# Attention and mixture of adapters in one kernel: the order of the work written out as one list

## The chip, the cores and the metric

The kernel runs on one core of a Trainium2 chip. The core has a matrix engine (PE, with its weight loads shown apart as PEld), a vector engine (DVE), a scalar engine (ACT), GpSimd (POOL) and SyncE (SP), which only issues DMAs here; sixteen DMA engines move data. Each engine works through its own instructions strictly in order, and semaphores order engines against each other. The metric is the device time of one execution in microseconds. Matmuls write to PSUM, from where DVE or ACT copy ("evict") to SBUF.

## The reference

```
q, k, v: 8 batches x 8 heads x 576 rows x 64
phi(x)  = [max(x,0) * cos(pos), max(x,0) * sin(pos)]          # 128 features
kv      = phi(k)^T v            (per batch and head, 128 x 64)
z       = sum of phi(k) over the rows
attn    = (phi(q) kv) / (phi(q) z + 1e-6)
x       = attn as 4608 tokens x 512
logits  = x @ w_gate            (8 experts)
w       = softmax over the two largest logits
out     = x + sum over those two of w * ((x @ A[e]) @ B[e])   # rank 16
```

## The kernel before, in words

The 4608 tokens are cut into 36 tiles of 128. Nine tiles (`NS` is 9) belong to two batches: four to the first, one, the mixed tile, half to each, four to the second. A batch's k, q and v each come with one DMA that also turns float32 into bfloat16; these loads are issued on POOL's queue, except the first k, which SP issues. There are five buffers each for q and v; from batch 5 on, k, q and v reuse the earlier ones.

Work per batch: 9 columns s of k are scaled by the cosine and the sine (18 products `kp`), on DVE (L153), ACT (L151) or POOL (L156). DVE and ACT take the maximum with 0 in the same instruction; for POOL's columns DVE applies it beforehand, in place (`relu_k`, L165), and POOL waits for that. `kv` (L180) then adds up the 9 columns in two PSUM tiles `cd`, 8 matmuls a column, and `kv_out` (L188) copies the sum to SBUF.

Work per tile n: `transp_q` transposes and scales q by matmuls with diagonal matrices, as 16 matmuls (L213), or for some tiles as 32 small ones ("quad", L201); `evac_q` evicts the two halves with the maximum (L229 on ACT, L231 on DVE). `numden` (L257) multiplies them with kv into the one PSUM tile `nd`; 1e-6 is added by two small matmuls (L252), or, where `eps_dve(n)` says so, by DVE in `normalise` (L268). `normalise` takes the reciprocal (L270) and multiplies (L277) into `xt`. `transp_x` (L285) transposes `xt` into the PSUM tile `xz`, `evac_x` (L291) copies it to SBUF as `xT`, `logits` (L311) multiplies it with A and w_gate. `nd` and `xz` are single: the next tile's `numden` waits for this tile's multiplication, the next `transp_x` for this tile's copy.

Work per group of three tiles: `gate_a` (L320 to L328) finds the two largest logits, `gate_sig` (L337) takes a sigmoid on ACT, `gate_b` (L344, L346) weights the rank-16 products into `zg`; `transp_z` (L359) transposes them into the second half of `xz`, and they are copied with the next xT, or by `evac_z`. Then for each tile `delta` adds two products in PSUM, x itself (L377) and the adapters' part (L382); `evac_o` (L408 on ACT, L410 on DVE) copies to `osb`, which has 24 buffers, and `store` issues one DMA on SP (two for a mixed tile). In `delta_add` (L397, L402) x is added by POOL in SBUF, in place of the product L377.

The order is that of the Python program, since the framework keeps each engine's instructions in the order written. A loop over the tiles writes one fixed pattern per tile; tables filled ahead of it (`kv_at`, `relu_at`, `pool_at`, `act_at`, `dve_at`, `early_at`, `late_at` and others) say at which tile a column, a relu or a group's step is written. For batches 2 to 7 all of POOL's columns of one batch stand in one block behind the relus that they need, and the loads of later batches behind that block: k of b+3, q of b+2, v of b+3. The small DMA `first_loads` on SP reads one row of the last batch's k; every store stands behind it on SP's queue, and the last batch's relu, which overwrites that buffer, waits for it.

Of the kernel before, what the change touches and what calls it, by code (L numbers as in the profile page):

```python
# [15 lines left out]
EPS = 1e-6  # L16


@with_exitstack
def kernel(ctx, tc, q, k, v, w_gate, A, Bw, out):  # L20
# [169 lines left out]
    def quad(n):  # L190
        return n >= 27

    def transp_q(n):
# [14 lines left out]
        for gp in range(2):  # L208
            qpT_t[n, gp] = t = qd.tile([128, 2, 4, HALF], FP32, name="qd", tag="qd")
            for j, (b, s) in enumerate(tokens(n)):  # L210
                for gi in range(2):
                    for i, cols in enumerate((lo, hi)):
                        nc.tensor.matmul(out=t[cols, j, 2 * gi:2 * gi + 2, :],  # L213
                                         lhsT=q_b[b][:, 2 * gp + gi, s, :], rhs=diag[:, s, i],
                                         start=(j == 0 and gi == 0), stop=True,
                                         skip_group_check=True)
# [16 lines left out]
    def move_q(n):  # L233
        transp_q(n)
        evac_q(n, 0)
        evac_q(n, 1)

    def eps_dve(n):

        return n > 13 and n in kv_at  # L240
# [46 lines left out]
    def evac_x(n, g=None):  # L287
# [3 lines left out]
        nc.vector.tensor_copy(t[:, 0:c], xz[:, 0:c * 128].rearrange("p (c s) -> p c s", c=c))  # L291
# [69 lines left out]
    def evac_z(g, parts):  # L361
        zgT_t[g] = t = p_g.tile([128, 3, 128], BF16, name="zgT")
        for eng, i, j in parts:
            if eng == "act":
                nc.scalar.copy(t[:, i:j], zT_ps(g)[:, i:j])
            else:
                nc.vector.tensor_copy(t[:, i:j], zT_ps(g)[:, i:j])
# [16 lines left out]

    def delta(n, own=True):
        delta_x(n, own)
        delta_z(n)

    def delta_add(n, own=True):

        if own:
            dx = cd[dx_n[0] % 2]
            dx_n[0] += 1
        else:
            dx = qd.tile([128, DM], FP32, name="dx", tag="qd")
        g = group_of[n]
        nc.tensor.matmul(out=dx, lhsT=zgT_t[g][:, n - groups[g][0], :], rhs=Ball,  # L397
                         start=True, stop=True)
        osb_t[n] = dx
        evac_o(n)  # L400
# [22 lines left out]

    kv_at, relu_at, pool_at, act_at, dve_at = {}, {}, {}, {}, {}

    def put(at, step, what):
        at.setdefault(step, []).append(what)

    for s in range(NS):
        for i in range(2):  # L430
            put(act_at if s % 2 == 0 and s < 8 else dve_at, 1 if s < 4 else 2, (1, s, i))
    kv_at[2] = [(1, s) for s in (1, 0, 3, 2)]
    kv_at[3] = [(1, s) for s in (5, 4, 7, 8, 6)]
    for b in range(2, B):
        first = b // 2 * NS + b % 2 * 4
        at = {2: 5, 3: 8, 4: 12, 5: 17, 6: 20, 7: 23}[b]
        n_pool = {2: 5, 3: 7, 4: 8, 5: 8}.get(b, 9)
        for s0, s1 in ((0, 3), (3, n_pool)):
            put(relu_at, at, (b, s0, s1))
        for s in range(n_pool):  # L440
            put(pool_at, at, (b, s))
        for i in range(2):
            if n_pool <= 7:
                put(dve_at, at, (b, 7, i))
            if n_pool < 9:
                put(act_at, first - 4 + i, (b, 8, i))
            if n_pool == 5:
                put(act_at, first - 3 + i, (b, 6, i))
                put(act_at, first - 2, (b, 5, i))
        order = (7, 0, 1, 2, 3, 4, 8, 6, 5) if n_pool <= 7 else (0, 1, 2, 3, 4, 5, 8, 6, 7)  # L450
        if n_pool == 9:
            order = range(NS)
        for j, s in enumerate(order):

            if b == 2:
                ahead = 2 if j < 4 else 1
            elif b == 3:
                ahead = 3 if j < 2 else 2 if j < 5 else 1
            else:
                ahead = 4 - min(j // 2, 3)  # L460
            put(kv_at, first - ahead, (b, s))

    early_at, late_at, gate_a_at, gate_b_at, move_at = {}, {}, {}, {}, {}
    prev = 5
    for g, t in enumerate(groups[:-2]):
        at = max(t[-1] + 1, prev + 1)
        for n in t:
            if t[-1] + 1 < at or (n < t[-1] and prev == at - 1):  # L470
                put(late_at, at - 1, n)
            else:
                put(early_at, max(n + 1, at - 1), n)
        prev = at + 1
        put(gate_a_at, at, g)
        put(gate_b_at, at + 1, g)
        put(move_at, at + 2, g)
    put(late_at, NT - 2, NT - 3)

    with tc.manual_schedule():  # L480
# [19 lines left out]
        load_v(3)  # L500
        load_k(4)
        load_q(3)
# [7 lines left out]
        g10, g11, g12 = range(len(groups) - 3, len(groups))  # L510
        todo, held = [], []
        first_loads = persist.tile([1, 8], BF16, name="first_loads")

        def emit(d, own=True, eng="act", add=False):
            if add:
                delta_add(d, own)
            else:
                delta(d, own)
                evac_o(d, eng)
            if held is None:  # L520
                store(d)
            else:
                held.append(d)

        for n in range(NT - 1):
            if n > 0:
                g = move_at.get(n - 1, (None,))[0]
                evac_x(n - 1, g)
                if g is not None:
                    todo += groups[g]  # L530
            normalise(n)
            if n != 3:
                move_q(n + 1)
            for b, s in kv_at.get(n, ()):
                kv(b, s)
                if kv_n[b] == NS:
                    kv_out(b)
            for t in early_at.get(n, ()):
                logits(t)
            if n == 3:  # L540
                move_q(n + 1)
            for g in gate_a_at.get(n, ()):
                gate_a(g)
            for g in gate_b_at.get(n, ()):
                gate_b(g)
            now = todo[:2 if len(todo) > 3 and n not in kv_at else 1]
            del todo[:len(now)]
            for d in now:
                emit(d, n not in kv_at, add=n > 27)
            for g in gate_a_at.get(n, ()):  # L550
                gate_sig(g)
            transp_x(n)
            for g in move_at.get(n, ()):
                transp_z(g)
            for b, s, i in dve_at.get(n, ()):
                scale_k1(b, s, i, "dve")
            for b, s0, s1 in relu_at.get(n, ()):
                relu_k(b, s0, s1)
            for b, s in pool_at.get(n, ()):
                scale_k(b, s)  # L560
                if (b, s) == pool_at[n][-1]:
                    if b + 3 < B:
                        load_k(b + 3)
                    if b + 2 < B:
                        load_q(b + 2)
                    if b + 3 < B:
                        load_v(b + 3)
                    if b + 3 == B - 1:

                        nc.sync.dma_start(out=first_loads, in_=k_b[B - 1][0:1, 0, 0, 0:8])  # L570
                        for d in held:
                            store(d)
                        held = None
            for t in late_at.get(n, ()):
                logits(t)
            numden(n + 1)
            for b, s, i in act_at.get(n, ()):
                scale_k1(b, s, i, "act")


        evac_x(NT - 2)
        normalise(NT - 1)
        transp_z(g10)
        logits(NT - 2)
        evac_z(g10, [("act", 0, 3)])
        todo += groups[g10]
        for d in todo[:-3]:
            emit(d)
        transp_x(NT - 1)
        gate_a(g11)  # L590
        emit(todo[-3])
        gate_sig(g11)
        evac_x(NT - 1)
        logits(NT - 1)
        gate_b(g11)
        emit(todo[-2])
        gate_a(g12)
        transp_z(g11)
        evac_z(g11, [("act", 0, 2)])
# [36 lines left out]
```

## Time and profile before

| | |
|---|---|
| median of 3 runs | 114.68 us (114.47 to 114.92) |
| the profiled execution | 114.54 us |
| its span, first to last instruction | 112.8 us |
| granted PE clock | 0.996 |
| read from HBM, written to it | 28.85 MB, 9.44 MB |

In the profile, a row of a group reads: line, engine, operation, output<-inputs, shapes and count, then busy time in us, mean ns of one, and the idle time before it with what ended it. A row of the timeline reads: start in us, length in us, engine, line, operation, and in brackets idle time before it. A row with "x2" covers two instructions; starts can lie closer together than lengths, since an engine begins an instruction before the last has quite ended. In the chain of waits a row is a start, a length and what ran or was waited for.

### The profile page before, as it was taken

The page shows a single profiled execution, that of the slowest core. Times are in us where ns is not written, and L with a number is a line of the kernel's source. Part 1 is how long each engine was busy: PE and PEld are TensorE (multiplying, and loading weights), DVE is VectorE, ACT ScalarE, POOL GpSimd, SP SyncE. Part 2 cuts the span into 40 slices and gives each one's busy share as a digit, 9 for nine tenths or more (in the row PEclk, how much of TensorE's full clock was granted, in tenths as well). Part 3 has the DMA queues.
Part 4 walks back from the last instruction along what each step waited for, and adds up shares of the span by engine and source line. Part 5 has one row for each costly group of instructions (what it writes and reads, how often), then busy time and mean ns, then how long its engine had stood idle before and what let it go on. Part 6 is the DMA issues. An engine that isn't in the chain of part 4 may idle for free.

```text
span 112.8 us, 4956 instructions
## 1 busy us (share of the span) xinstructions
PE 96.1 (85%) x2050; PEld 74.1 (66%) x2068; DVE 83.7 (74%) x296; ACT 78.2 (69%) x169; POOL 72.3 (64%) x134
## 2 busy tenths in 40 slices
PE   2999676978899899999999999998998997978710
PEld 1347465867796788868788888785786886754200
DVE  5598489459969677695987998999949589786620
ACT  5087579755986595797876978856777777895720
POOL 5992223228995996299939999989980445774000
PEclk9999999999999999999999999999999999999998
DMA  2999999999999999999999999999999424526892
GB/s 41 385 206 208 213 202 210 210 180 208 208 208 209 207 209 209 209 206 213 204 207 208 208 209 208 242 348 383 381 324 366 142 100 97 185 101 226 285 340 82
DMA packets 19670, 24.77 MB, mean 220 GB/s; under 512 B 2624, under 2 KB 14528, under 8 KB 19648
## 3 DMA queue, kind: packets, MB, share of 16 engines
q0 software_dynamic: 13856, 13.84, 73.8%
q1 hardware_dynamic: 5792, 10.62, 26.9%
q8 instruction: 16, 0.26, 0.9%
q14 instruction: 6, 0.05, 0.1%
HBM read 28.85 MB, written 9.44 MB: 340 GB/s over the span
## 4 chain that ended last, share of the span: by engine, by line
PE 40%; DMA 28%; DVE 15%; issue 4%; POOL 4%; ACT 4%; POOLq 0%; DVEq 0%; ACTq 0%
DMA k<-in_k_dram 14%; DMA v<-in_v_dram 12%; PE cd L180 9%; PE za L311 7%; PE qd L213 6%; PE xz L285 5%; PE nd L257 4%; DVE xt L277 4%; PE dx L377 3%; DVE k L165 3%; DVE xT L291 2%; DVE zg L346 2%; ACT osb L408 2%; PE qd L201 2%; DMA out_dram<-osb 2%
## 5 line engine op out<-in xcount | busy, mean ns | idle before, releaser
L229 ACT ACTIVATE qpT<-qd 128x512 bf16<-128x512 f32 x71 | 38.6, 595 | 15.0 <-PE qd L213 10.9
L156 POOL TENSOR_SCALAR kp<-k,cos_tab 128x256 bf16<-128x256 bf16 x46 | 22.6, 490 | 7.1 <-DVE k L165 6.5
L277 DVE TENSOR_TENSOR xt<-nd,rden 128x512 bf16<-128x512 f32 x36 | 24.9, 691 | 1.3
L291 DVE COPY xT<-xz 128x512 bf16<-128x512 bf16 (+1 forms) x36 | 17.1, 476 | 9.9 <-PE xz L359 6.4
L156 POOL TENSOR_SCALAR kp<-k,sin_tab 128x256 bf16<-128x256 bf16 x46 | 21.9, 476 | 0.0
L180 PE MATMUL cd<-v,kp 64*128 64x128 bf16 x576 | 20.3, 217 | 0.9 <-DVE kp L153 0.9
L285 PEld LDWEIGHTS <-xt 128*128 128x128 bf16 x144 | 10.8, 115 | 12.1 <-DVE xt L277 7.9
L285 PE MATMUL xz<-ident,xt 128*128 128x128 bf16 x144 | 14.4, 222 | 5.0 <-DVE xt L277 4.3
L180 PEld LDWEIGHTS <-kp 64*128 64x128 bf16 x576 | 16.3, 94 | 3.1 <-issue 0.9
L257 PE MATMUL nd<-kvsb,qpT 128*128 128x65 bf16 (+1 forms) x320 | 16.7, 195 | 1.1 <-DVE qpT L231 0.5
L213 PE MATMUL qd<-diag,q 128*64 128x128 bf16 x432 | 17.3, 222 | 0.3 <-DMA q<-in_q_dram 0.3
L402 POOL TENSOR_TENSOR osb<-osb,xt 128x512 f32<-128x512 f32 x8 | 9.2, 1160 | 9.6 <-ACT osb L408 8.0
L408 ACT COPY osb<-dx 128x512 f32<-128x512 f32 x19 | 11.2, 588 | 5.9 <-remote 2.1
L213 PEld LDWEIGHTS <-q 128*64 128x64 bf16 x432 | 13.1, 109 | 1.8 <-DMA q<-in_q_dram 0.5
L257 PEld LDWEIGHTS <-qpT 128*128 128x128 bf16 (+1 forms) x320 | 12.7, 100 | 1.9 <-ACT qpT L229 0.7
L311 PE MATMUL za<-AW,xT 128*128 128x144 bf16 x140 | 12.4, 227 | 0.7 <-DVE zg L346 0.5
L311 PEld LDWEIGHTS <-xT 128*128 128x128 bf16 x144 | 9.0, 98 | 3.2 <-DVE xT L291 1.0
L408 ACT COPY osb<-cd 128x512 f32<-128x512 f32 x16 | 9.1, 597 | 1.3 <-PE cd L382 1.3
L62 POOL DMA_DIRECT2D v<-in_v_dram x8 | 6.2, 778 | 5.2 <-DMA q<-in_q_dram 4.4
L485 PE MATMUL wu<-wide,ones 128*128 128x512 bf16 x24 | 7.3, 477 | 2.0 <-DVE AW L115 2.0
L62 POOL DMA_DIRECT2D q<-in_q_dram x8 | 6.1, 763 | 3.6 <-DMA k<-in_k_dram 3.6
L62 POOL DMA_DIRECT2D k<-in_k_dram x7 | 5.4, 771 | 3.9 <-DMA k<-in_k_dram 2.2
(75 smaller groups left out, 133.8 us busy)
## 6 DMA issues: line engine op xcount, KB each, us to landing
out_dram<-osb SPq DMA_DIRECT2D x32, 256.0 KB, 3.9
v<-in_v_dram POOLq DMA_DIRECT2D x8, 576.0 KB, 16.5
q<-in_q_dram POOLq DMA_DIRECT2D x8, 576.0 KB, 15.6
k<-in_k_dram POOLq DMA_DIRECT2D x7, 576.0 KB, 15.5
k0f<-in_k_dram SPq DMA_DIRECT2D x1, 1152.0 KB, 5.4
out_dram<-osb SPq DMA_DIRECT2D x8, 128.0 KB, 2.4
AW<-in_moe_A_dram POOLq DMA_DIRECT2D x1, 128.0 KB, 18.2
Ball<-in_moe_B_dram POOLq DMA_DIRECT2D x1, 128.0 KB, 16.7
```

What stands on the lines that cost most here:

```text
L62: eng.dma_start(out=t, in_=rows(dram, b))
L156: nc.gpsimd.tensor_scalar(out=dst, in0=src, scalar1=tab, scalar2=1.0, op0=ALU.mult, op1=ALU.mult)
L180: nc.tensor.matmul(out=kvz[par][:, g], lhsT=kp_t[b][pr, s, g], rhs=v_rhs(b, g, s, pr), start=(first and g == 0), stop=(last and g == G - 1))
L213: nc.tensor.matmul(out=t[cols, j, 2 * gi:2 * gi + 2, :], lhsT=q_b[b][:, 2 * gp + gi, s, :], rhs=diag[:, s, i], start=(j == 0 and gi == 0), ...
L229: nc.scalar.activation(t, src, AF.Relu)
L257: nc.tensor.matmul(out=nd[pr, gg, j * W:(j + 1) * W], lhsT=qpT[:, j, pr], rhs=kv_t[b][:, h % 2, h // 2, :], start=(eps_dve(n) and j == 0), ...
L277: nc.vector.tensor_tensor(out=x, in0=nd[:, :, :, 0:D], in1=rden.rearrange("p (g j) -> p g j", g=2).to_broadcast([128, 2, 4, D]), op=ALU.mult)
L285: nc.tensor.transpose(out=xz[:, c * 128:(c + 1) * 128], in_=x[:, c], identity=ident)
L291: nc.vector.tensor_copy(t[:, 0:c], xz[:, 0:c * 128].rearrange("p (c s) -> p c s", c=c))
L311: nc.tensor.matmul(out=za_t[g][:, i, :], lhsT=xT[:, c, :], rhs=AW[:, :, c, :], start=(c == 0 and i == 0), stop=(c == DCH - 1), skip_group_ ...
L402: nc.gpsimd.tensor_tensor(out=t, in0=t, in1=xt_t.pop(n), op=ALU.add)
L408: nc.scalar.copy(t, src)
```

## The change

The loop and its tables go. In their place stands a string, `ORDER`, of 673 steps; one line of Python runs through it and calls the function of each letter. Since an engine's instructions keep the order written, the string is at the same time the list of each engine. The letters: R normalise, N numden, X transp_x, L logits, O delta, V evac_o, P the addition of x on POOL, T store, A gate_a, S gate_sig, B gate_b, Z transp_z, Y evac_z, Q transp_q, E evac_q, C evac_x, W kv_out, M kv (batch.column), K one product of a column (batch.column.cosine or sine.engine), G both products of a column on POOL, U relu_k (batch.first.end), D a load (k, q or v of a batch). The engine is a last letter a (ACT) or d (DVE).

What is done stays the same, with these differences of place: the tiles whose 1e-6 is added on DVE (`EPS_DVE`, 25 for 16), the quads (`QUAD`, 7 for 9), the tiles to which POOL adds x (`ADDS`, 8 for 8, others); products of k columns for batches 1 to 7 are 36 on ACT (20 before), 26 on DVE (14) and 64 on POOL (92); 7 evictions of q are on DVE (1 before), 6 output copies on DVE (1), 9 copies of xT on ACT (none). A tile's two halves of q can be transposed at different places. The loads behind v of batch 4 come as k5, k6, q4, v5, q5, k7, v6, q6, v7, q7 (before k5, q4, v5, k6, q5, v6, k7, q6, v7, q7), and q3 ahead of k4.

```diff
+EPS_DVE = [1, 2, 3, 5, 6, 7, 10, 11, 14, 17, 18, 20, 21, 22, 23, 24, 25, 26, 27, 28, 29, 30, 31, 33, 35]
+QUAD = [28, 29, 30, 31, 33, 34, 35]
+ADDS = [14, 20, 21, 22, 23, 26, 27, 28]
+ORDER = """
+R0 Q1.0 Q1.1 E1.0.a E1.1.a Q2.0 N1 E2.0.a X0 R1 Q2.1 Q3.0 K1.0.0.a E2.1.a C0.d K1.4.1.a K1.7.0.d
...
+N6 U2.0.3 X5 K2.8.0.d E7.1.a G2.0 U2.3.4 Q8.0 R6 K2.4.0.a Q8.1 E8.0.a L1 G2.1 L2 C5.d K2.6.0.a
+N7 A0 K2.6.1.a X6 Dk.5 M2.1 K2.5.1.a R7 M2.8 C6.a M2.4 G2.2 M2.0 S0 M2.5 E8.1.a M2.6 B0 X7 G2.3
+N8 K2.7.0.d C7.d L3 L4 R8 L5 Q9.0 Q9.1 A1 E9.0.a M2.2 M2.3 E9.1.d M2.7 S1 Q10.0 W2 B1 X8 Z0
+E10.0.a N9 C8.d.0 K3.5.0.a Q10.1 R9 Q11.0 E10.1.a L6 O0 K3.6.1.a K3.8.1.d N10 U3.0.3 K3.6.0.a X9
+U3.3.5 G3.0 R10 E11.0.a Q11.1 L7 E11.1.a L8 G3.1 K3.7.0.a O1 A2 V0.a Z1 N11 G3.2 V1.a C9.d.1
+Q12.0 Q12.1 K3.5.1.a R11 X10 G3.3 E12.0.a M3.6 M3.0 S2 M3.5 E12.1.d M3.2 Dk.6 M3.1 C10.d Q13.0
+Q13.1 G3.4 B2 E13.0.a N12 K3.7.1.a E13.1.d X11 Dq.4 O2 K3.8.0.d L9 R12 V2.a Z2 M3.4 C11.a M3.3
+M3.7 K4.5.1.d M3.8 U4.0.3 L10 U4.3.5 W3 G4.0 K4.6.0.d L11 K4.7.0.d X12 A3 O3 G4.1 N13 K4.8.1.d
+S3 K4.7.1.d V3.a B3 G4.2 Q14.0 C12.a.2 Q14.1 R13 O4 E14.0.a Dv.5 O5 E14.1.a V4.d L12 G4.3 X13
+N14 V5.d C13.a Q15.0 Q15.1 Dq.5 R14 E15.0.a M4.7 M4.2 M4.1 K5.7.0.a M4.0 K5.8.1.d E15.1.a O6
+U5.0.3 X14 G5.0 V6.a N15 C14.d K5.7.1.a Q16.0 U5.3.7 G5.1 Q16.1 R15 E16.0.a L13 Z3 E16.1.a L14
+G5.2 K5.8.0.d O7 K4.5.0.d Y3.a A4 O8 V7.a G4.4 N16 K4.8.0.d V8.a K6.8.0.d X15 K4.6.1.d K6.4.1.a
+Q17.0 U6.0.3 G5.3 Q17.1 R16 E17.0.a M4.8 M4.3 S4 M4.5 G5.4 E17.1.a C15.d M4.6 M4.4 B4 Q18.0 W4
+Dk.7 Q18.1 N17 E18.0.a Z4 G5.5 X16 R17 E18.1.a O9 K6.5.1.a Q19.0 G6.0 Q19.1 K6.6.1.a C16.d N18
...
+E19.0.a O10 R18 Dv.6 E19.1.a X17 L15 K6.7.0.a G5.6 Q20.0 Q20.1 C17.d V9.a N19 E20.0.a G6.1 L16
+R19 X18 E20.1.a L17 V10.a G6.2 Q21.0 Q21.1 C18.d E21.0.a N20 A5 X19 Dq.6 E21.1.a M5.4 R20 M5.3
+S5 C19.a.4 M5.0 Dv.7 M5.5 O11 K6.5.0.a K6.8.1.d N21 K6.6.0.a O12 U7.0.3 K7.7.1.a M5.1 U7.3.7
+V11.a G7.0 M5.6 V12.d M5.8 M5.2 M5.7 B5 G7.1 Q22.0 T0 W5 Q22.1 R21 L18 E22.0.a T1 X20 Z5 E22.1.a
+O13 T2 U6.3.4 C20.d.5 O14 V13.a N22 T3 K7.8.0.a Q23.0 R22 Q23.1 T4 E23.0.a L19 L20 E23.1.a X21
+A6 O15 V14.a T5 Q24.0 C21.d Q24.1 P14 S6 K6.7.1.a T6 N23 B6 X22 E24.0.a O16 T7 R23 E24.1.a G7.2
...
+E35.0.a B10 E35.1.a P28 X34 T27 N35 C34.a Z10 L33 R35 Y10.a L34 T28 V29.a O30 A11 T29 X35 V30.a
+O31 C35.d S11 T30 V31.a B11 L35 A12 T31 Z11 O32 Y11.a S12 O33 V32.a B12 V33.a T32 Z12 O34 Y12.d
+O35 T33 V34.a V35.d T34 T35
+"""
...
     def quad(n):
-        return n >= 27
+        return n in QUAD
...
     def eps_dve(n):
-        return n > 13 and n in kv_at
+        return n in EPS_DVE
...
-        nc.vector.tensor_copy(t[:, 0:c], xz[:, 0:c * 128].rearrange("p (c s) -> p c s", c=c))
+        copy = nc.vector.tensor_copy if eng == "dve" else nc.scalar.copy
+        copy(t[:, 0:c], xz[:, 0:c * 128].rearrange("p (c s) -> p c s", c=c))
...
+    def delta(n):
+        if any(0 < c < NS or c == NS and b not in kv_t for b, c in kv_n.items()):
+            dx = qd.tile([128, DM], FP32, name="dx", tag="qd")
+        else:
+            dx = cd[dx_n[0] % 2]
+            dx_n[0] += 1
+        g = group_of[n]
+        if n not in ADDS:
+            nc.tensor.matmul(out=dx, lhsT=ident, rhs=xt_t.pop(n), start=True, stop=False)
+        nc.tensor.matmul(out=dx, lhsT=zgT_t[g][:, n - groups[g][0], :], rhs=Ball,
+                         start=n in ADDS, stop=True)
         osb_t[n] = dx
...
         load_k(3)
         load_v(3)
+        load_q(3)
         load_k(4)
-        load_q(3)
         load_v(4)
...
+        for op in ORDER.split():
+            do[op[0]](*(int(a) if a.isdigit() else a for a in op[1:].split(".")))
```

More of the change, by code (lines that the diff above doesn't have):

```diff
@@ L421, in store @@
             (eng or nc.sync).dma_start(out=dst, in_=t)
[L424 to L478, printed above, removed]
     with tc.manual_schedule():
@@ L508 @@
         numden(0)
-        g10, g11, g12 = range(len(groups) - 3, len(groups))
-        todo, held = [], []
         first_loads = persist.tile([1, 8], BF16, name="first_loads")
[L514 to L578, printed above, removed]
@@ L581 @@
[L581 to L599, printed above, removed]
-        gate_sig(g12)
```

83 lines of the change are left out of this document (40 added, 43 removed).

## The prediction

> **What bounds the kernel now.** The page comes first: no engine is full over the span.
>
> ```profile
> span 112.8 us, 4956 instructions
> PE 96.1 (85%) x2050; PEld 74.1 (66%) x2068; DVE 83.7 (74%) x296; ACT 78.2 (69%) x169; POOL 72.3 (64%) x134
> ```
>
> Then the stages, from the windows view (columns: length, busy time of PE, PEld, DVE, ACT and POOL with counts, granted clock, DMA share, GB/s).
>
> ```profile
> 34.40:50.00 15.60, 14.61 (x299) 11.66 (x303) 12.12 (x42) 11.06 (x26) 11.58 (x23) 1.00 1.21 207
> 50.00:72.00 22.00, 21.61 (x446) 17.64 (x449) 18.02 (x61) 17.24 (x38) 20.21 (x42) 1.00 1.21 208
> 55.27:102.08 46.81, 44.02 (x1071) 35.87 (x1081) 38.88 (x127) 35.58 (x77) 34.95 (x64) 1.00 0.89 231
> ```
>
> The reader sees two things. To 72 us the loads run at one steady rate, 207 to 208 GB/s. From 34.4 us on PE is covered almost wholly, and DVE is busy for 38.9 of 46.8 us between tile 16 and tile 35. The chain of waits says the same in order of time: loads of k and v to 34.4 us, then PE.
>
> ```profile
> 18.76 15.64 DMA k<-in_k_dram
> ...
> 34.42 0.48 DVE kp L153 x2
> ```
>
> The third load of k lands at 18.76 + 15.64 = 34.40. The table of issues gives the size of a load:
>
> ```profile
> k<-in_k_dram POOLq DMA_DIRECT2D x7, 576.0 KB, 15.5
> out_dram<-osb SPq DMA_DIRECT2D x8, 128.0 KB, 2.4
> ```
>
> 576 KB are 0.590 MB, at 207 GB/s 2.85 us a load. The order in which loads are issued therefore fixes when each can land, whatever the engines do.
>
> **Where a tile stands.** I mark a tile by the start of its multiplication (L277, R in the list). The timeline of DVE has them, and with them the prices of DVE work by the distance of starts.
>
> ```profile
> 47.90 0.20 DVE L270 RECIPROCAL rden<-nd 128x8 f32<-128x8 f32 x1
> 48.13 0.69 DVE L277 TENSOR_TENSOR xt<-nd,rden 128x512 bf16<-128x512 f32 x1
> 48.74 0.17 DVE L344 TENSOR_TENSOR em<-za,mask 128x24 f32<-128x24 f32 x1
> 48.94 0.56 DVE L346 TENSOR_TENSOR zg<-za,em 128x384 bf16<-128x384 f32 x1
> 49.42 0.41 DVE L291 COPY xT<-xz 128x512 bf16<-128x512 bf16 x1
> 49.75 0.15 DVE L268 TENSOR_SCALAR den<-nd 128x8 f32<-128x8 f32 x1
> 49.94 0.20 DVE L270 RECIPROCAL rden<-den 128x8 f32<-128x8 f32 x1
> 50.18 0.69 DVE L277 TENSOR_TENSOR xt<-nd,rden 128x512 bf16<-128x512 f32 x1
> ...
> 53.09 0.69 DVE L277 TENSOR_TENSOR xt<-nd,rden 128x512 bf16<-128x512 f32 x1
> 53.85 0.32 DVE L320 MAX8 m<-za 128x8 f32<-128x8 f32 x3
> ...
> 54.50 0.42 DVE L291 COPY xT<-xz 128x512 bf16<-128x512 bf16 x1
> ...
> 55.27 0.69 DVE L277 TENSOR_TENSOR xt<-nd,rden 128x512 bf16<-128x512 f32 x1
> ```
>
> Tiles 13 to 16 stand at 48.13, 50.18, 53.09 and 55.27. Prices: multiplication 0.61 (48.13 to 48.74), gate_b 0.68 (48.74 to 49.42), copy of xT 0.33, reciprocal 0.23, reciprocal with the addition of EPS 0.43, gate_a 0.65 (53.85 to 54.50). Tile 35, from which the tail hangs:
>
> ```profile
> 70.80 0.69 DVE L277 TENSOR_TENSOR xt<-nd,rden 128x512 bf16<-128x512 f32 x1
> ...
> 102.08 0.69 DVE L277 TENSOR_TENSOR xt<-nd,rden 128x512 bf16<-128x512 f32 x1
> ```
>
> The first row is tile 22. Behind tile 35 stand the same gates in both kernels, seven deltas before and six after, and the last stores; I take that tail as unchanged.
>
> **The change, part by part.** *PE work.* The list takes EPS on DVE in 25 tiles, before in 16: 18 fewer matmuls of L252. It makes two fewer tiles in quads (7 for 9).
>
> ```profile
> 47.09 0.11 PE nd L252
> ...
> 49.54 0.57 PE qd L213 x16
> ```
> ```profile
> 83.48 0.46 PE qd L201 x32
> ```
>
> 18 x 0.11 = 2.0 us less at most, 2 x (0.57 - 0.46) = 0.2 us more, and 9 x 0.20 = 1.8 us more on DVE. Eight tiles are added on POOL in both kernels. Of PE's 96.1 busy us, under 2 go.
>
> *PE order.* The matmuls of tile n+1 (N) no longer wait behind a fixed pattern; transpositions (X), logits (L) and deltas (O) are spread so that 1.3 to 2 us of them lie between one N and the next. With that cover the waits for L277 mostly go, and the DMA sets the pace: q3 is now loaded ahead of k4 and lands at 34.40 + 2 x 2.85 = 40.1, k4 at 42.95, k5 at 48.65.
>
> *Columns of k.* From 92 operations on POOL to 64; ACT has 36 for batches 1 to 7 where it had 20, DVE 26 where it had 14. POOL was hidden before and stays so; ACT has room (35.6 of 46.8 us busy in the third window). Each moved column costs DVE 0.24 (0.48 for two at 34.42), 2.9 us for twelve.
>
> *Evictions, copies, additions.* Six more evictions of q (E) and five more output copies (V) go to DVE, about 0.61 each, 6.7 us; nine copies of xT (C) go to ACT, 3.0 us less on DVE. With EPS and the columns DVE gains some 8 us on 83.7, ACT about 5 on 78.2:
>
> ```profile
> L229 ACT ACTIVATE qpT<-qd 128x512 bf16<-128x512 f32 x71 | 38.6, 595 | 15.0 <-PE qd L213 10.9
> ```
> ```profile
> L151 ACT ACTIVATE kp<-k,cos_tab 128x256 bf16<-128x256 bf16 x10 | 5.1, 508 | 0.0
> ```
>
> Five of the eight additions on POOL come earlier, where only stores wait for them. On POOL's queue k6 and k7 are issued ahead of q4 and v6, still several loads ahead of their turn; on SP's, the stores stand behind first_loads as before and start when k7 lands. None of this is on the path, as long as DVE keeps up.
>
> *DVE among POOL's columns.* Before, DVE touched k in SBUF (L153, L165) almost only while POOL stood waiting for it. The list puts columns and relus (K, U) of DVE among POOL's columns. What that costs is shown by one place of the trace where it already happens:
>
> ```profile
> 73.57 2.36 DVE L165 TENSOR_SCALAR k<-k 128x768 bf16<-128x768 bf16 x2
> 75.85 0.61 DVE L291 COPY xT<-xz 128x896 bf16<-128x896 bf16 x1
> ```
> ```profile
> 73.41 0.48 POOL L156 TENSOR_SCALAR kp<-k,cos_tab 128x256 bf16<-128x256 bf16 x1
> ...
> 74.77 0.49 POOL L156 TENSOR_SCALAR kp<-k,sin_tab 128x256 bf16<-128x256 bf16 x1
> 75.75 0.53 POOL L156 TENSOR_SCALAR kp<-k,cos_tab 128x256 bf16<-128x256 bf16 x1 [0.49 <-PE qd L213]
> ```
> ```profile
> 46.70 0.75 DVE L165 TENSOR_SCALAR k<-k 128x768 bf16<-128x768 bf16 x2
> 47.37 0.61 DVE L291 COPY xT<-xz 128x896 bf16<-128x896 bf16 x1
> ```
>
> Two relus beside an idle POOL pass in 0.67 us (46.70 to 47.37). The same two, dispatched at 73.57 among four POOL columns, took 2.28: the next instruction started at 75.85, after POOL's run had ended at 75.26. POOL's columns kept their pace of 0.455 (73.41 to 74.77 in three). So DVE stood still until POOL's whole run was over. [...]
>
> Now the list is followed on DVE, an in-order queue, from k4 on. *Tile 13*: a column, two short relus and two columns (42.95 + 0.24 + 0.45 + 0.48 = 44.1), gate_a (44.75). K4.8.1 and K4.7.1 then meet POOL's six columns, begun at 44.1 and over at 44.1 + 6 x 0.455 = 46.85. The two columns run beside the next DMA issue; there a column took up to 0.51, so 0.35 each:
>
> ```profile
> 26.35 0.51 DVE L153 TENSOR_SCALAR kp<-k,sin_tab 128x256 bf16<-128x256 bf16 x1
> ```
>
> 47.55; gate_b 48.25; reciprocal: tile 13 at 48.5, 0.35 late. N13 was done before and PE has only some 1.7 us of cover, so X13 and N14 wait for it. *Tile 14*: two output copies moved to DVE, priced as the multiplication, 2 x 0.61, then 0.43: 50.75, 0.6 late. *Tile 15*: a column, the relu U5.0.3 (from 51.6), copy of xT to 52.2; POOL has begun eight columns at 52.05, which end at 55.7; U5.3.7 stands behind them, 0.35, then 0.23: 56.3, 3.2 late. *Tile 16*: four POOL columns to 57.95, two DVE columns beside the issue of k7 (0.7), gate_a 0.65 to 59.3, POOL to 59.6, three columns and a relu 1.0, reciprocal 0.23: 60.85, 5.6 late.
>
> *Tile 16 to 35.* Before took 46.81. Its blocked relu goes (2.28 - 0.67 = 1.6), leaving 45.2. The floor is DVE's own busy time in that stretch, 38.9. With two-tile look-ahead I take the middle, 42.2. One block remains: U6.3.4 behind POOL's columns of batch 7, about 1.2. Sum 43.4: tile 35 at 104.25, 2.2 late. The profiled execution took 114.54 us (span 112.8), within 0.14 of the median 114.68. **Forecast: 114.54 + 2.2 = 116.8 us.** Its own range: 114.4, if the stretch comes near its floor, to 119.6, at 45.2 and with one more such block.
>
> **The rivals.** *First: DVE waits for one column only.* Then each of some 12 operations costs at most 0.45, most of it under cover. k5 lands at 48.65, ACT's column (0.51) and eviction (0.60) follow, so tile 15 stands at about 50.5, 2.6 early; the 17.7 us before took from there to tile 22 shrink to about 17, which is 67.5. But another wait stands there: the relu U7.0.3 writes k's last buffer and so waits for the little read first_loads, issued when k7 lands at 48.65 + 5 x 2.85 = 62.9. A store lands in 2.4 us where it is alone; those issued while loads were still queued took longer:
>
> ```profile
> DMA to landing us min/median/max: 6.4/7.2/7.7
> ```
>
> That row is for the stores issued from 67 to 70 us. Between 2.4 and 6.4 I take 4.4: 67.3. Two relus 0.67, an output copy 0.61, gate_b 0.68, 1.04 for tile 21, then N22 and 0.85: tile 22 at 71.2, where before has 70.80. From there before took 31.28; less 1.6, and 0.7 for the look-ahead, 29.0: tile 35 at 100.2, 1.9 early, **112.7 us** (110.7 to 114.7 with the two landings). The trace speaks for first_loads' price and against the short wait.
>
> *Second: neither wait binds.* If first_loads lands unnoticed as well, tile 22 stands at 67.5 and the end is 114.54 - (70.8 - 67.5) - 2.3 = **109 us**. For it speaks only that the DMA order allows it.
>
> *Third: it does nothing.* Look-ahead and blocks cancel, 114.5 us; they would have to agree within 0.6.
>
> **How the numbers follow.** Forecast 0.56, first rival 0.26, second 0.11, third 0.07. Half a per cent, 0.57 us, is about what a measurement of this kernel can tell from no change. Slower by more: nearly all of the forecast and a little of the first, 0.57. Faster: most of the first, all of the second, a little of the forecast, 0.35. Within: 0.08. Range 110.8 to 119.6: it leaves out the second rival's lower half and the worst of the forecast.
>
> **What would show it.** In the changed kernel's timeline of DVE, U5.3.7 and K4.8.1 (the relu and scale_k1 lines) of 2 us and more, each ending with a run of POOL's columns; tile 15 after 55 us. If instead those rows are below 1 us, the first rival holds, and the longest wait of DVE must be the relu of batch 7 for a DMA. A tile 16 before 54 us would prove the sum wrong at its root. The PE waits for L277 should be fewer behind tile 22 than before.

## The result, and the profile after

The changed kernel takes 119.42 us (median of four runs, 119.06 to 119.47) where the kernel before takes 114.58: a ratio of 1.041 [1.038, 1.044]. It is 4.8 us slower; the forecast was 2.2 us slower, with 119.6 as the upper end. The ratios here and below leave out executions more than 1.5% above the fastest of their kernel. The profiled execution took 119.41 us. The head of its page, with the clock and the rate of the DMAs in 40 slices of 2.94 us:

```profile
span 117.5 us, 4896 instructions
...
PE 99.5 (85%) x2018; PEld 73.3 (62%) x2018; DVE 88.5 (75%) x321; ACT 84.1 (72%) x185; POOL 59.6 (51%) x106
...
PEclk9999999999999999999999975699999999999998
...
GB/s 47 382 207 207 207 210 206 192 201 208 207 210 207 210 206 208 207 212 204 204 165 194 192 199 285 391 392 329 127 249 213 105 0 95 274 230 218 227 344 62
```

Two things are new. The granted clock falls in three slices, from 67.6 to 76.4 us, and PE's busy time has grown by 3.4 us (96.1 before) though no matmul was added. The third of the windows below goes from tile 16 to tile 35, as the third one shown of before did:

```profile
34.40:50.00 15.60, 15.20 (x324) 11.94 (x323) 15.03 (x51) 12.58 (x29) 11.46 (x22) 1.00 1.21 207
50.00:72.00 22.00, 17.10 (x363) 13.29 (x357) 14.48 (x52) 16.28 (x38) 15.07 (x30) 0.93 1.18 202
55.53:106.82 51.29, 44.51 (x1008) 33.73 (x1003) 37.80 (x130) 37.91 (x83) 26.31 (x43) 0.93 0.87 214
```

To 50 us PE is covered as well as before. Then the loss comes all at once: in the second window PE is busy for 17.1 of 22 us (21.61 before), at a clock of 0.93. The chain of waits names the place:

```profile
56.96 7.46 DMA k<-in_k_dram
64.51 5.14 DMA first_loads<-k
69.74 0.70 DVE k L214 x2
```

The last k, issued at 56.96, landed at 64.4. The little read of 16 bytes took 5.14 us, and the relu of batch 7 (L214) waited for it on DVE. The timeline of DVE shows who stood behind that relu:

```profile
63.37 0.69 DVE L321 TENSOR_TENSOR xt<-nd,rden 128x512 bf16<-128x512 f32 x1
...
69.74 0.70 DVE L214 TENSOR_SCALAR k<-k 128x768 bf16<-128x768 bf16 x2 [5.49 <-DMA first_loads<-k]
70.35 0.68 DVE L438 COPY osb<-dx 128x512 f32<-128x512 f32 x1
70.95 0.17 DVE L389 TENSOR_TENSOR em<-za,mask 128x24 f32<-128x24 f32 x1
...
72.06 0.69 DVE L321 TENSOR_TENSOR xt<-nd,rden 128x512 bf16<-128x512 f32 x1
...
78.69 0.69 DVE L321 TENSOR_TENSOR xt<-nd,rden 128x512 bf16<-128x512 f32 x1
...
106.82 0.69 DVE L321 TENSOR_TENSOR xt<-nd,rden 128x512 bf16<-128x512 f32 x1
```

These are tiles 20, 21, 23 and 35. V12 (L438), B5 (L389) and tile 21 stood behind the relu. V12 empties the PSUM buffer `dx`, which Q22 takes next, so PE stood still as well; its timeline:

```profile
66.32 0.41 PE L262 MATMUL qd<-diag,q 128*64 128x128 bf16 x8
71.09 0.64 PE L262 MATMUL qd<-diag,q 128*64 128x128 bf16 x8 [4.36 <-DVE osb L438]
```

Windows of 1 us (the last three columns are granted clock, DMA share and GB/s) show what PE's standstill left behind:

```profile
68.00:69.00 1.00, 0.00 (x0) 0.00 (x0) 0.00 (x0) 0.00 (x0) 0.00 (x0) 0.98 1.18 184
69.00:70.00 1.00, 0.00 (x0) 0.00 (x0) 0.26 (x1) 0.00 (x0) 0.00 (x0) 0.50 1.08 164
...
75.00:76.00 1.00, 1.00 (x21) 0.83 (x16) 0.87 (x3) 0.49 (x2) 0.00 (x0) 0.61 1.06 396
76.00:77.00 1.00, 1.00 (x14) 0.64 (x11) 0.64 (x6) 1.00 (x3) 0.00 (x0) 1.00 1.11 406
```

The clock is halved from 68.96 (0.98 is 0.04 us at half) to 75.78 (0.61 is 0.78 us at half): 6.8 us, of which PE worked 4.7. It fell 2.2 us after PE's last matmul had ended (66.32 + 0.41). What sets the start and the length of the stretch is not shown.

For the account, the same tiles of the kernel before:

```profile
65.26 0.69 DVE L277 TENSOR_TENSOR xt<-nd,rden 128x512 bf16<-128x512 f32 x1
...
68.31 0.69 DVE L277 TENSOR_TENSOR xt<-nd,rden 128x512 bf16<-128x512 f32 x1
...
72.96 0.69 DVE L277 TENSOR_TENSOR xt<-nd,rden 128x512 bf16<-128x512 f32 x1
```

| stretch | before | after | difference |
|---|---|---|---|
| start to tile 20 | 65.26 | 63.37 | -1.89 |
| tile 20 to 21 (the wait) | 3.05 | 8.69 | +5.64 |
| tile 21 to 23 (half clock) | 4.65 | 6.63 | +1.98 |
| tile 23 to 35 | 29.12 | 28.13 | -0.99 |
| tile 35 to the end | 10.72 | 10.68 | -0.04 |

The sum is 4.70, the difference of the spans. The list was 1.9 us ahead at tile 20, and one wait with its consequence cost 7.6.

### The profile page after: what moved, and what is told of

It reads as the page before. It is cut to its first block, busy times and chain, and to the rows that moved or that the text cites. A ratio compares the mean times of both kernels' runs of the same rounds, so it can differ in the third digit from the quotient of the medians.

```text
span 117.5 us, 4896 instructions
## 1 busy us (share of the span) xinstructions
PE 99.5 (85%) x2018; PEld 73.3 (62%) x2018; DVE 88.5 (75%) x321; ACT 84.1 (72%) x185; POOL 59.6 (51%) x106
## 4 chain that ended last, share of the span: by engine, by line
PE 47%; DVE 28%; DMA 11%; ACT 4%; issue 3%; POOL 3%; DVEq 0%; ACTq 0%; SPq 0%
PE cd L229 9%; DVE xt L321 7%; PE wu L456 7%; DMA k<-in_k_dram 6%; PE qd L262 6%; PE za L356 5%; PE nd L301 5%; PE xz L329 5%; DMA first_loads<-k 4%; DVE xT L336 4%; DVE kp L202 3%; DVE zg L391 3%; POOL kp L205 3%; PE cd L423 2%; ACT qpT L278 2%
## 5 line engine op out<-in xcount | busy, mean ns | idle before, releaser
L278 ACT ACTIVATE qpT<-qd 128x512 bf16<-128x512 f32 x64 | 36.2, 601 | 11.7 <-PE qd L262 10.7
L321 DVE TENSOR_TENSOR xt<-nd,rden 128x512 bf16<-128x512 f32 x36 | 24.9, 692 | 1.5
L262 PE MATMUL qd<-diag,q 128*64 128x128 bf16 x464 | 20.4, 227 | 5.3 <-DVE osb L438 4.4
L205 POOL TENSOR_SCALAR kp<-k,cos_tab 128x256 bf16<-128x256 bf16 x32 | 15.7, 490 | 14.4 <-DVE k L214 6.4
L262 PEld LDWEIGHTS <-q 128*64 128x64 bf16 x464 | 14.9, 112 | 8.9 <-issue 6.6
L229 PE MATMUL cd<-v,kp 64*128 64x128 bf16 x576 | 19.4, 217 | 0.5 <-DMA v<-in_v_dram 0.5
L205 POOL TENSOR_SCALAR kp<-k,sin_tab 128x256 bf16<-128x256 bf16 x32 | 15.4, 481 | 0.0
L436 ACT COPY osb<-cd 128x512 f32<-128x512 f32 x21 | 12.0, 595 | 2.1 <-PE cd L423 2.0
L336 DVE COPY xT<-xz 128x512 bf16<-128x512 bf16 (+1 forms) x27 | 12.1, 447 | 1.8 <-PE xz L329 1.2
L200 ACT ACTIVATE kp<-k,cos_tab 128x256 bf16<-128x256 bf16 x18 | 8.9, 506 | 0.0
L200 ACT ACTIVATE kp<-k,sin_tab 128x256 bf16<-128x256 bf16 x18 | 8.7, 509 | 0.0
```

The lines of the kernel that those rows point to most:

```text
L200: nc.scalar.activation(dst, src, AF.Relu, bias=0.0, scale=tab)
L205: nc.gpsimd.tensor_scalar(out=dst, in0=src, scalar1=tab, scalar2=1.0, op0=ALU.mult, op1=ALU.mult)
L229: nc.tensor.matmul(out=kvz[par][:, g], lhsT=kp_t[b][pr, s, g], rhs=v_rhs(b, g, s, pr), start=(first and g == 0), stop=(last and g == G - 1))
L262: nc.tensor.matmul(out=t[cols, j, 2 * gi:2 * gi + 2, :], lhsT=q_b[b][:, 2 * gp + gi, s, :], rhs=diag[:, s, i], start=(j == 0 and gi == 0), ...
L278: nc.scalar.activation(t, src, AF.Relu)
L321: nc.vector.tensor_tensor(out=x, in0=nd[:, :, :, 0:D], in1=rden.rearrange("p (g j) -> p g j", g=2).to_broadcast([128, 2, 4, D]), op=ALU.mult)
```

## The experiments

Base is the changed kernel or, where the text says "with the moved read", the first experiment's kernel.

**1. The little read looks elsewhere.**

```diff
-                nc.sync.dma_start(out=first_loads, in_=k_b[b][0:1, 0, 0, 0:8])
+                nc.sync.dma_start(out=first_loads, in_=k_b[b][0:1, G - 1, NS - 1, 0:8])
```

> The changed kernel with one edit: the little DMA first_loads reads 16 bytes of column 8 of the last k, which no relu writes, in place of column 0. It still waits for the landing of that k, and the stores still stand behind it, but the relu U7.0.3 no longer waits for it. Theory W (the wait for first_loads decides): the relu starts when k7 lands, at about 64.5 us, and tile 21 stands at about 64.5 + 0.67 + 0.61 + 0.68 + 1.04 = 67.5, some 4.5 us earlier than 72.06; the time falls from 119.4 to about 114.9, and to about 113.5 if the low granted clock behind the stall goes with it. Rival L (DVE's columns and relus among POOL's columns, or the order as a whole, make it slow): tile 21 moves by under 1 us and the time stays above 118.4.

Measured: 115.04 us, ratio to before 1.006 [1.004, 1.009]. DVE's timeline at the same place:

```profile
64.91 0.70 DVE L214 TENSOR_SCALAR k<-k 128x768 bf16<-128x768 bf16 x2 [0.28 <-DMA k<-in_k_dram]
65.58 0.69 DVE L438 COPY osb<-dx 128x512 f32<-128x512 f32 x1
...
67.30 0.69 DVE L321 TENSOR_TENSOR xt<-nd,rden 128x512 bf16<-128x512 f32 x1
...
72.36 0.69 DVE L321 TENSOR_TENSOR xt<-nd,rden 128x512 bf16<-128x512 f32 x1
...
102.00 0.69 DVE L321 TENSOR_TENSOR xt<-nd,rden 128x512 bf16<-128x512 f32 x1
```

5.49 us of waiting became 0.28, tile 21 stands 4.8 us earlier, and 4.4 us of the loss are gone with one address. Theory W held. Tiles 21 to 23 take 5.06 us here and 6.63 in the changed kernel, so the half clock, with the work that had piled up, was worth 1.6. But the lead of 1.5 us at tile 20 (63.75) is gone at tile 35: 102.00, as before. Something else takes it.

**2. The relus of batch 7 later in the list.**

```diff
-O12 U7.0.3 K7.7.1.a M5.1 U7.3.7 V11.a G7.0 M5.6 V12.d M5.8 M5.2 M5.7 B5 G7.1 Q22.0
+O12 M5.1 V11.a M5.6 V12.d M5.8 M5.2 M5.7 B5 Q22.0
...
-R23 E24.1.a G7.2
+R23 U7.0.3 U7.3.7 K7.7.1.a E24.1.a G7.0 G7.1 G7.2
```

> The changed kernel with the relus of batch 7 (U7.0.3, U7.3.7) and the columns G7.0 and G7.1 that need them written behind tile 23, ahead of G7.2. first_loads reads what it read. Theory W: V12, B5 and tile 21 no longer stand behind any DMA on DVE; tile 21 at about 66 us (63.37 of tile 20 and 2.5 us), 6 us earlier; the relus then stand at about 70.5, when first_loads has landed (69.7) or nearly; the time is 112.5 to 114. Rival L: above 118. Rival K (the landing of k7 and first_loads come later in this order, or the columns of batch 7 come late for kv): the stall appears again behind tile 23 with over 2 us, and the time is 115 to 118.

Measured: ratio 1.002 [0.998, 1.006], ten executions from 113.48 to 117.23 us. The second way to take the wait away gives the same as the first, less than expected, and no new wait for the read appears (rival K). The row of PE's waits that remains points to the rest:

```profile
PE nd L301 <- issue: 2.0, 1, 2.0
```

PE waits for nothing that the profile shows, once, for 2 us, in the middle of eight matmuls. The first experiment's kernel has the like, in its timeline of PE:

```profile
43.76 1.01 PE L229 MATMUL cd<-v,kp 64*128 64x128 bf16 x30 [0.79 <-issue]
...
85.11 0.23 PE L301 MATMUL nd<-kvsb,qpT 128*128 128x65 bf16 x2
86.79 0.35 PE L301 MATMUL nd<-kvsb,qpT 128*128 128x65 bf16 x6 [1.46 <-issue]
```

In the kernel before, no row of PE's waits ends with "issue".

**3. With the moved read, no quads** (`QUAD = []`).

> The kernel with the moved read, and no tile as a quad (QUAD is empty): the seven late tiles transpose q with 16 matmuls each, not 32 small ones, so PE has 7 x 32 fewer instructions and 7 x 0.11 = 0.8 us more of matmul time. Theory I (PE runs out of its own code: the blocks of 16384 bytes on the instruction queue come at 84.53 and 88.74, and PE stands still from 85.3 to 86.8 in the middle of eight matmuls of nd, and from 90.6 to 91.1): both gaps go, tile 35 stands 0.7 to 1.5 us earlier than 102.0 and the time is 113.5 to 114.3. Rival Q (the gaps are a wait for q, for an eviction or for a store that the trace does not name): the gap of 1.46 stays, and the time is 115.0 to 116.0.

Measured: 113.02 us, ratio 0.988 [0.983, 0.992]. The two gaps behind 85 us (1.46 and, at 91.07, 0.51) are gone; PE's waits of that kind are down to

```profile
PE qd L262 <- issue: 0.3, 1, 0.3
...
PE xz L329 <- issue: 0.2, 1, 0.2
```

That is 2.0 us less than with quads. The gaps account for 1.97 - 0.54 = 1.4 and the longer matmuls give back 0.8, so 0.6 was to be expected; between tile 23 (71.98) and tile 35 (100.51) the trace has 28.5 us where the first experiment has 29.6. Tile 23 itself stands 0.4 earlier (72.36 with the moved read), where the gap of 0.79 at 43.76 is missing; the rest I did not trace.

**4. With the moved read, PE's code lengthened by half a block.**

```diff
+        for i in range(64):
+            nc.tensor.matmul(out=wu[:, 0:16], lhsT=ones, rhs=wide[:, 0:16], start=True, stop=True)
```

> The kernel with the moved read, and 64 matmuls of 16 columns more in the warm-up, where PE waits for the first load anyway. They lengthen PE's code by 128 instructions, half a block of 16384 bytes, and change nothing else. Theory I (PE waits for its own code): the gap behind the second of eight matmuls of nd at 86.8 us is not there any more; a gap of 0.3 to 2 us stands at another instruction, 128 instructions of PE earlier or later, or none where PE works slowly enough; the blocks on the instruction queue come at other times. The time is 114 to 116. Rival Q (a wait for data): the gap of 1.46 stays at the same matmuls of nd of tile 29.

Measured: ratio 1.004 [1.001, 1.007]. The gap at tile 29's matmuls is not there; in the same stretch PE now stops at other instructions:

```profile
85.94 0.35 PE L250 MATMUL qd<-diag,q 64*64 64x64 bf16 x20 [1.00 <-issue]
...
90.74 0.46 PE L229 MATMUL cd<-v,kp 64*128 64x128 bf16 x10 [0.83 <-issue]
```

Counting PE's instructions in the program as built, waits and branches included, the gaps of this kind of 0.2 us and more behind 70 us stand 255, 256 or 512 instructions apart where a kernel has several, and in all of them at 194 or 195 modulo 256:

```
kernel                gap at us   instruction   modulo 256
changed                 92.17        3266          194
moved read              86.79        3266          194
moved read              91.07        3522          194
relus later             86.96        3266          194
half a block longer     73.55        2755          195
half a block longer     85.94        3267          195
half a block longer     90.74        3522          194
no quads                80.53        3011          195
no quads                86.94        3266          194
```

In the lengthened kernel, 3267 is another matmul (one of a quad). So PE ran out of code at a border of blocks: theory I holds, and a wait for data falls. The transfers on the instruction queue say the same: the page of the changed kernel has 16 packets and 0.26 MB on it for 4036 matmuls and weight loads, 252 to a packet of 16384 bytes, and each of the nine gaps ends 1.2 to 1.6 us after such a block has landed (with the moved read at 85.48 and 89.65, for 86.79 and 91.07). That quads use up a block faster than the next one comes is likely, since 32 small matmuls and as many weight loads pass in 0.46 us, but it is not the whole reason: the gap at 43.76 stands among the matmuls of `kv`. A gap cost 0.2 us (no quads) to 2.0 us (relus later).

**5. With the moved read, quads for tiles 33 to 35 alone.**

> The kernel with the moved read and quads only for tiles 33, 34 and 35. By theory I the gaps at 86.8 and 91.1 belonged to the quads 28 to 31, so they stay away, and three quads save 3 x 0.11 us of PE: 112.6 to 113.2, as the kernel without quads or 0.3 less; a gap near the last quads would show in PE's idle time instead.

Measured: 112.71 us, ratio 0.983 [0.980, 0.987], the lowest median of this study, though its interval overlaps the one without quads. One gap of 0.79 remains, at instruction 3011, ahead of all quads:

```profile
80.64 0.25 PE L329 MATMUL xz<-ident,xt 128*128 128x128 bf16 x1 [0.79 <-issue]
```

**6. The kernel before without quads** (`return n >= 36`).

> The kernel before with no tile as a quad (nine before). Its trace shows no wait of PE for code. Theory I: nothing to gain, nine tiles cost 9 x 0.11 = 1.0 us more on PE, of which some is hidden: 114.5 to 115.5. If quads were slower in themselves, it would be below 114.

Measured: 114.16 us, ratio 0.997 [0.996, 0.998], between the two answers. Nine quads cost 0.3% there, seven cost 1.8% in the changed list (1.006 to 0.988). That their crowding in the changed list is what costs is not shown: in the kernel before PE got through 256 instructions in 4.6 us (90.8 to 95.4, quads among them) without a gap, while the gaps at 43.76 (moved read) and 80.64 (experiment 5) came after 256 instructions in 6.2 and 6.1 us. What makes a block late stays open.

**7. The changed kernel with quads for tiles 33 to 35, its wait kept.**

> The changed kernel with quads for tiles 33, 34 and 35 alone; the wait for first_loads stays. The standstill at 67 to 71 and the low clock stay; the gap of 0.88 us at 92.2 goes. If the prices add, the time is 119.4 - 0.9 - 4 x 0.11 = 118.1; if PE's lateness hid the missing code, 119.0 to 119.4.

Measured: 118.72 us, ratio 1.042 [1.034, 1.049]. The gap of 0.88 is gone and the standstill is 4.8 us. The four executions, 118.07, 118.60, 118.83 and 120.37, reach from the one answer to beyond the other: inconclusive on whether the prices add.

**8. A standstill without a DMA.** With the moved read; eight and four copies between the relus.

```diff
-U7.0.3 K7.7.1.a M5.1 U7.3.7
+U7.0.3 K7.7.1.a M5.1 H8 U7.3.7
...
+        def hold(n):
+            for i in range(n):
+                nc.vector.tensor_copy(fill[:, i % 4 * DM:(i % 4 + 1) * DM], xz[:, 0:DM])
```

> The kernel with the moved read, and eight copies of 128x512 from PSUM on DVE between the two relus of batch 7 (nobody uses what they write). They take 8 x 0.6 = 4.8 us and hold V12, B5 and tile 21 as long as first_loads did, without any wait for a DMA. Theory G (PE's standstill itself lowers the granted clock): the clock falls to 0.5 some 2 us after PE stops and stays there for 6 us, as in the changed kernel; tile 21 at about 72, tile 23 at 78 to 79, the time 119 to 120, that is more than the 4.8 us that were put in less what is hidden. Rival D (the low clock came with the DMA traffic of those microseconds, or by chance): the clock stays above 0.98, tile 23 at 72.4 + 4.7 = 77.1, the time 117.5 to 118.8.

> As the kernel with eight copies, with four: 2.4 us. Theory G: PE stands still for about 2 us; that is shorter than what lowered the clock for 6 us, so the clock falls not at all or for one stretch of 3 us; the time is 116.5 to 118. If the price of a standstill were only its length, it would be 115.0 + 2.0 = 117.0 in every run alike.

Measured: eight copies 119.31 us, ratio 1.040 [1.034, 1.046], the changed kernel's own; four copies 1.024 [1.018, 1.031]. The long one's windows:

```profile
69.00:70.00 1.00, 0.00 (x0) 0.00 (x0) 1.00 (x3) 0.00 (x0) 0.00 (x0) 0.76 1.07 176
...
75.00:76.00 1.00, 1.00 (x10) 1.00 (x9) 0.24 (x1) 1.00 (x3) 0.00 (x0) 0.50 1.09 358
76.00:77.00 1.00, 1.00 (x12) 0.56 (x12) 0.94 (x7) 0.31 (x3) 0.76 (x1) 0.83 1.07 374
```

Theory G held: half clock from 69.5 to 76.3, again 6.8 us, with no wait for a DMA; PE had stood still for 2.9 us at a stretch. Three of its four executions had a mean clock of 0.953 to 0.955 and took 119.29 to 119.86; one had 0.981, at most 4.4 us at half (0.019 x 116.3 x 2), and took 118.11, so 6.8 us are not paid every time. What they cost stays open: here over a microsecond, but the changed kernel's execution with a mean clock of 0.980, at most 4.7 us at half (0.020 x 117.6 x 2), took 119.47, as long as the others. With four copies PE stood still for 1.5 us in the profiled execution and kept its clock (1.00 in each window from 68 to 73 us); over its executions the mean clock went from 0.961 to 0.992.

**9. DVE's columns ahead of POOL's run.** With the moved read.

```diff
-K4.5.1.d M3.8 U4.0.3 L10 U4.3.5 W3 G4.0 K4.6.0.d L11 K4.7.0.d X12 A3 O3 G4.1 N13 K4.8.1.d S3 K4.7.1.d
+K4.5.1.d K4.8.1.d K4.7.1.d M3.8 U4.0.3 L10 U4.3.5 W3 G4.0 K4.6.0.d L11 K4.7.0.d X12 A3 O3 G4.1 N13 S3
...
-K5.8.1.d E15.1.a O6 U5.0.3
+K5.8.1.d K5.8.0.d K4.5.0.d K4.8.0.d K4.6.1.d E15.1.a O6 U5.0.3 U5.3.7
```

> The kernel with the moved read, and DVE's columns and relus of batches 4 and 5 written ahead of POOL's run and not among its columns: K4.8.1 and K4.7.1 next to K4.5.1 ahead of U4.0.3; K5.8.0, K4.5.0, K4.8.0 and K4.6.1 ahead of U5.0.3, and U5.3.7 right behind U5.0.3. Theory R (the prediction's, DVE starves among POOL's columns): tiles 13 to 16 stand much earlier than in the changed kernel (tile 13 before 46.5, tile 16 before 54). Theory C (each waits for one column at most): some 0.25 us less for each of six columns, so tile 13 0.5 us and tile 16 1 to 1.5 us earlier (before 55); the end moves by less than that, 114.0 to 115.0. If they cost nothing beyond their own time, tile 16 stays at 55.5 to 56.

Measured: ratio 1.000 [0.997, 1.003]. Tile 16 stands at 54.46 for 55.91 with the moved read alone, 1.45 earlier, as theory C had it; tile 13 gains 0.2 and tile 17 nothing (58.06 for 57.96). What DVE loses among POOL's columns is small, and PE takes it back within a tile. The total says less: this kernel's profiled execution lost 3.5 us to gaps of PE's code behind tile 23 (1.07, 1.11 and 1.34), against 2.0 with the moved read alone.

**10. The lock by itself.** Three tails behind the changed kernel's last step, and one move in the kernel before.

> The changed kernel with a tail behind its last step, which computes nothing that is stored: 27 columns of k on POOL, back to back, and beside them on DVE, each behind two copies from PSUM of 0.6 us, relus of 128x768 and 128x1536 and columns of 128x256; then the same DVE instructions again when POOL is done. Theory R (the prediction's: DVE stands still until POOL's whole run is over): the first relu lasts until POOL's run ends, some 10 us. Theory C (DVE waits for the one column that runs): each lasts its own time (about 0.25, 0.35 and 0.55) and at most 0.46 more, and POOL's columns next to them last up to 0.6 longer. Theory M (it is decided anew at each border of two columns): most are as in C, some wait for two to four columns, up to 1.9 us.

> The changed kernel with another tail that computes nothing that is stored: 45 columns of k on POOL back to back, and on DVE 16 relus of 128x768 and columns of 128x256 in turn, each behind a copy of 0.6 us and one of 64, 88, ... 424 elements, so that they begin at ever other points of POOL's column. Theory C: every one of them lasts at most 0.46 us more than alone (0.35 and 0.28). Theory M: some wait for several columns, as the relu of the kernel before at 73.57 did (1.90 us). Theory R (until POOL's run is over) fell for the changed kernel's own columns; if it held here for a relu, that would last over 5 us.

> The changed kernel with a third tail, which computes nothing that is stored: 36 columns of k on POOL in the kernels' own layout, cosine and sine in turn, and on DVE eight times a multiplication like that of a tile, a relu of 128x768, one of 128x1536 and a copy of 64 to 400 elements; then, with nothing else going on, the little read of 16 bytes on SP and a relu that waits for it as U7.0.3 does. If the pair behind a multiplication starves, some of the eight first relus last 0.9 to 1.9 us; if not, all last at most 0.35 + 0.46. The little read: if its 5.14 us come from the loads queued at that time, DVE waits 2 to 2.6 us here; if they belong to the read, 5 us again.

> The kernel before with the two relus of batch 7 written ahead of the division of tile 23, some 1.1 us earlier on DVE, when POOL still has 6 columns of its run to do (they end at 75.25). If the starving belongs to POOL's unbroken run, the first relu begins at about 72.5 and lasts until 75.4, 2.9 us, and tile 23 stands 3 us later. If a relu waits for one column only, as in the changed kernel, it lasts 0.35 to 0.65, and the pair is over by 73.6.

Measured, in one execution of each: in the first tail all six lasted as long beside POOL as alone (0.35, 0.28, 0.55), and POOL paid (0.51 to 0.86 for the column beside them, 0.47 alone). If they had fallen in step with POOL's borders, that would say little, so the second tail varied the distance. Its timeline of DVE:

```profile
119.96 0.27 DVE L527 TENSOR_SCALAR wide<-k,cos_tab 128x256 bf16<-128x256 bf16 x1
...
121.04 0.58 DVE L214 TENSOR_SCALAR k<-k 128x768 bf16<-128x768 bf16 x1
...
122.44 0.50 DVE L527 TENSOR_SCALAR wide<-k,cos_tab 128x256 bf16<-128x256 bf16 x1
...
123.79 0.65 DVE L214 TENSOR_SCALAR k<-k 128x768 bf16<-128x768 bf16 x1
```

Its sixteen relus and columns lasted 0.35 to 0.65 and 0.27 to 0.52: at most 0.30 more than alone, never a second column. The eight pairs of the third tail show the same (first relu 0.34 to 0.58). Theory C holds. In the kernel before, with the pair moved into the middle of POOL's run, both relus together took 1.38, where the prediction's reading asks for 2.9 for the first alone:

```profile
72.45 1.38 DVE L165 TENSOR_SCALAR k<-k 128x768 bf16<-128x768 bf16 x2
```

At its old place, in the kernel before without quads, it starved again:

```profile
73.54 2.29 DVE L165 TENSOR_SCALAR k<-k 128x768 bf16<-128x768 bf16 x2
```

So the row on which I built belongs to that place and returns there; nowhere else in these runs was DVE seen to wait for more than one column. Why it does there stays open. The third tail's end has the little read with no load queued (POOL still works on its columns): issued at 126.28, and the relu waiting for it started at

```profile
128.12 0.43 DVE L214 TENSOR_SCALAR k<-k 128x768 bf16<-128x768 bf16 x1 [0.92 <-DMA quiet<-k]
```

1.84 us, against 5.14 while loads were queued: the difference of 3.3 us goes with the queued loads.

## Why the prediction was right or wrong

*Right side, wrong cause, so the side was luck.* Slower was forecast, but the step that gave the 2.2 us failed: "So DVE stood still until POOL's whole run was over." The prediction named its own test, U5.3.7 and K4.8.1 of 2 us and more. The changed kernel's rows:

```profile
44.23 0.48 DVE L202 TENSOR_SCALAR kp<-k,cos_tab 128x256 bf16<-128x256 bf16 x2
...
45.44 0.97 DVE L202 TENSOR_SCALAR kp<-k,sin_tab 128x256 bf16<-128x256 bf16 x2
...
51.46 0.45 DVE L214 TENSOR_SCALAR k<-k 128x1024 bf16<-128x1024 bf16 x1
51.83 0.19 DVE L314 RECIPROCAL rden<-nd 128x8 f32<-128x8 f32 x1
52.05 0.69 DVE L321 TENSOR_TENSOR xt<-nd,rden 128x512 bf16<-128x512 f32 x1
...
55.53 0.69 DVE L321 TENSOR_TENSOR xt<-nd,rden 128x512 bf16<-128x512 f32 x1
```

K4.8.1 and K4.7.1 took 0.97 where two columns alone take 0.48; U5.3.7 took 0.45. Tiles 13 to 16 stand at 47.24, 49.47, 52.05 and 55.53, where 48.5, 50.75, 56.3 and 60.85 were forecast: tile 16 was 0.3 us late, not 5.6. From there to tile 35 the sum had 43.4 us (its middle of 38.9 and 45.2 is 42.05, not 42.2, which changes little); the changed kernel took 51.3, and 46.1 with the moved read. In place of the step the runs show the wait for first_loads: 5.6 us at tile 21 and 2.0 behind it, and without it the ratio is 1.006. The first rival's reading, that DVE waits for one column only (at most 0.45 us, an estimate from POOL's column of 0.455), was weighed against one row and lost; every other row here agrees with it, and the second tail shows at most 0.30 us more than alone.

*The first rival had the mechanism, and its price was too small.* Its place was right: the relu of batch 7, waiting for first_loads, was DVE's longest wait, as it had said. Its terms were not. The last k landed at 64.4, not 62.9: it was issued behind twelve of POOL's columns at 56.96, when the load ahead of it was on its way and no other (q5 landed at 59.9), not several loads ahead of its turn as the prediction said; the slices from 59 to 71 us show 165 to 199 GB/s where 207 was assumed. The read took 5.14 us, not 4.4. And the rival let PE work on. It counted V12 behind the relu as 0.61 us of DVE, not as the copy that Q22 waits for, and so missed that PE would stand for 4.36 us and then run at half clock: from tile 21 to tile 22 it took 3.44 us, not 0.85. Tile 22 stands at 75.5, not 71.2. From there to tile 35 it took 31.3 us (29.0 by the rival, 31.28 before): the blocked relu did go, but of the 2.3 us that the rival took off for it and for the look-ahead, 1.0 was lost between tiles 22 and 23 (3.19 us for 2.16 before) and 0.88 in the gap at 92.17; the rest I did not trace.

*What held.* The last group of matmuls, gates and stores behind tile 35 is unchanged (10.72 and 10.68). PE's waits for a tile's multiplication went from 4.3 us in ten waits (L277) to 0.9 us in three (L321), behind tile 22 from 1.5 in four to 0.2 in one. DVE gained 4.8 us of work and ACT 5.9, where 8 and 5 were forecast. The loads landed as worked out up to the last k: k4 at 42.8 and k5 at 48.5.

*The second rival,* that neither wait binds, 109 us, is nearest to what was built in experiment 5: without the wait and with three quads it is 112.7. The window from tile 9 to tile 35 of that kernel:

```profile
35.32:100.40 65.08, 61.48 (x1330) 48.06 (x1342) 56.51 (x196) 54.33 (x119) 41.98 (x73) 1.00 1.05 234
```

PE is busy for 61.5 of 65.1 us in an execution of 112.27. The order of the DMAs allowed 109; that would leave PE 0.3 us of idle time in this window.

*The gain that was there.* The list had a lead of 1.9 us at tile 20, and it gains 1.7% at the end once both waits are taken out. One address gave away 4.4 us, and the list of seven tiles 2.0 to 2.3 more.

## What to carry to other kernels

When an order is rewritten, look for the instruction on an in-order queue that waits for a DMA, and price what stands behind it, PSUM buffers included: here a standstill of PE of 4.36 us cost its length and brought 6.8 us of half clock on top. A read that is meant as a signal should look at bytes that nobody will write. And one stretched row is a question, not a rate: before a sum is built on it, look for a second place that shows the same.

## What the runs showed of the hardware that was not expected

- PE waited for its own code: gaps of 0.2 to 2.0 us at places 255, 256 or 512 instructions apart (experiment 4), seen as "issue" in PE's waits, the nine listed there ending 1.2 to 1.6 us after a block of 16384 bytes had landed. The largest with the moved read (1.46) went when the quads of tiles 28 to 31 were taken out, but gaps of 0.8 us stand elsewhere too (0.79 at 43.76, and at 80.64 in experiment 5).
- The clock fell to half after some standstills of PE and not after others. One of 4.36 us brought 6.8 us of it (changed kernel), one of 2.9 us 6.8 too (experiment 8), one of 4.8 at most 4.0 (experiment 7: mean clock 0.983, 0.017 x 116.3 x 2), one of 1.46 at most 1.8 (experiment 1: 0.992, 0.008 x 112.6 x 2), one of 1.5 none from 68 to 73 us (four copies). A gap of 2.0 us for code (experiment 2) was enough for 3.4, from 88.2 to 91.6, 1.2 us after PE had gone on:

```profile
88.00:89.00 1.00, 1.00 (x49) 0.96 (x37) 0.97 (x3) 0.91 (x4) 0.00 (x0) 0.61 1.02 385
...
91.00:92.00 1.00, 1.00 (x37) 0.90 (x40) 0.84 (x3) 0.30 (x2) 0.69 (x1) 0.68 0.04 16
```

- The read of 16 bytes took 5.14 us behind queued loads (changed kernel) and 1.84 us with none queued (third tail).
- At one place of the kernel before, and only there, DVE waited through four of POOL's columns, in two kernels alike (2.36 and 2.29 us for the two relus, the second without quads); unexplained.
